# PE's matmuls in the attention loop: the scheduler's order or the source's

## The chip, the cores and the metric

The kernel runs on one core of a Trainium2 chip. The metric is the time of one execution on the device, in microseconds (us). Engines are named as in the profile: PE (matmul, with PEld for its weight loads), DVE (vector), ACT (scalar), POOL (GpSimd) and SP (DMA issue).

## The reference

Three stages follow one another: attention with pooled queries, a mixture of experts with top-1 routing and a skip rule, and a gated feed-forward layer.

```python
B, H, S, D = 4, 8, 1152, 64
q_pool = q.reshape(B, H, S // 2, 2, D).mean(axis=3)
scores = scale * q_pool @ k.transpose(0, 1, 3, 2)
attn = exp(scores - max(scores)); attn /= sum(attn) + 1e-9
x = (attn @ v), heads side by side            # 2304 x 512
x = x + gate * relu(x @ w1[e]) @ w2[e]        # rows with x @ w_skip > 0, e = argmax of x @ w_gate
out = (silu(x @ gate2) * (x @ val2)) @ out2   # d_ff 1536
```

All results are float32. To keep that precision on PE, operands of most products are split in a high and a low part (fp32r); the product with v and some small ones use plain fp32.

## The kernel before

Attention works on 16 pairs of heads, p = 0 to 15 (four pairs to a batch). For a pair, keys are cut in NC = 9 chunks of 128, queries (576 after pooling) in two halves n of 288, and a tile of scores is one (head, chunk, half).

The main loop, `for p in range(NP)` at line 786, is a software pipeline. It makes a list `main` of what pair p itself needs and a list `sides` of work for other pairs, and `spread` (line 24) emits both in one sequence: main pieces have whole positions, the pieces of a side are set evenly between two positions, and all are sorted.

Main pieces:

- `qk(p, h, c, n)`, lines 670 and 671: two fp32r matmuls (s) into a buffer of the PSUM pool ps_s (three buffers), then ACT's exp (line 674) into P[c], an SBUF tile with five buffers. In the source's order c runs from 0 to 8, and in a chunk (h, n) = (0,0), (0,1), then `values`, then (1,0), (1,1).
- `values`: for c = 2, 4, 6, 8 the products with v (`pv`, line 694, tile o) of chunks c-2 and c-1, eight fp32 matmuls; for c = 0 the four of the last chunk of the pair before. The matmul of head 0 writes partitions 0 to 63 and that of head 1 partitions 64 to 127, each a tile of 128x64 of PE, so the two can run side by side. At c = 4 the row sums of the pair before (`sums`, line 710, tile sm) come ahead of them.
- `evac(p - 1)`, line 702, on ACT after c = 0; `rowsum`, line 685, adds P to acc on POOL.

Side pieces:

- `m_pieces(p + 1)`: 27 score tiles of 128x384 for the row maxima (`m_tile`, mx, line 641), each reduced by DVE (line 643), and m_row, m_fin (mt, line 654, and line 655).
- `t_pieces(p + 2)`: transposes of k (tk, line 595, three at a time, copied out by ACT in lines 598 and 600) and of q (tq, line 608; lines 614 and 619 on ACT).
- `split_pieces(p + 3)`: the high and low parts of k and q (ACT and POOL), and its loads.
- In pairs from 4 on, Route: `rows(t)` (xr, lines 284 and 286; DVE lines 289 to 295; a store of the tile by SP, line 298; its SBUF tile xrs has one buffer), two tiles in pairs 4, 8, 12 and three in pairs 5, 9, 13; one-hot, softmax and rank in pairs 6, 10, 14 and near them, and scatters on POOL.
- In pairs 3 to 14, `Convert.decode` of weights stored as 64-bit floats (ACT lines 136 and 137, DVE lines 138 to 142), with a PSUM buffer; and in pair 15 the lists and loads for the experts, with the weight splits of lines 456 and 457.

mx, mt, tk, tq, sm, xr, and the PSUM tiles of decode and of the routing all take buffers of one pool, ps_m (three buffers); o has one tile of two banks of its own.

The instructions are emitted in this sequence, but Tile's scheduler sets the order on each engine: it plays the program through with its own cost model, and on each engine takes, of what it holds ready, the instruction emitted first. Where the next one in the source isn't ready by that model, a later one goes ahead. On the chip each engine then executes its list in order. Inside `tc.manual_schedule()` the order of emission is kept instead; the start of attention (`ramp`) and the experts (`moe`) are inside such regions, with all engines. The main loop isn't.

Of the kernel before, what the change touches and what calls it, by code (L numbers as in the profile page):

```python
# [20 lines left out]
ET = mybir.EngineType  # L21


def spread(main, sides):
    ev = []
    for i, f in enumerate(main):
        ev.append((i, 0, len(ev), f))
    for j, (pieces, a, b) in enumerate(sides):
        pieces = list(pieces)
        for i, f in enumerate(pieces):  # L30
            ev.append((a + (b - a) * (i + 0.5) / len(pieces), 1 + j, len(ev), f))
    for e in sorted(ev, key=lambda e: e[:3]):
        e[3]()
# [3 lines left out]
def body(ctx, tc, q, k, v, w_skip, w_gate, w1, w2, m2_gate, m2_val, m2_out, out):  # L37
# [433 lines left out]
    def attention(st):  # L471
# [186 lines left out]
        def m_pieces(p):  # L658
            r = [lambda i=i, j=j: m_tile(p, i // 5, i % 5, j) for i in range(9) for j in range(3)]
            r.insert(17, lambda: m_row(p, 0))  # L660
            r.insert(20, lambda: m_fin(p, 0))
            return r + [lambda: m_row(p, 1)]


        def qk(p, h, c, n):
            s = s_[p]
            cs = slice(c * 128, (c + 1) * 128)
            ns = slice(64 * h + n * 288, 64 * h + (n + 1) * 288)
            ps = ps_s.tile([128, 512], FP, tag="s", name="s")
            nc.tensor.matmul(ps[:, 0:288], s["ks"][:, h, cs], s["qsh"][:, h, ns], start=True, stop=False)  # L670
            nc.tensor.matmul(ps[:, 0:288], s["ks2"][0:69, h, cs], s["qsl"][0:69, h, ns], start=False, stop=True)  # L671
            if h == 0 and n == 0:
                s["P", c] = pp.tile([128, 2, 2, 288], FP, tag="P", name="P")
            i = nc.scalar.activation(s["P", c][:, h, n], ps[:, 0:288], AF.Exp, scale=0.5 / float(D) ** 0.5)  # L674
            if (h, c, n) == (0, 0, 0):
                mark[p] = i.ins.name

        def rowsum(p, c):
            s = s_[p]
            if c == 1:  # L680
                s["acc"] = accs[p % 2]
            if c:
                eng = nc.vector if p == last and c <= ACD else nc.gpsimd
                a = s["acc"][:].rearrange("p (h n c) -> p h n c", h=2, n=2)
                i = eng.tensor_tensor(a, s["P", 0][:] if c == 1 else a, s["P", c][:], op=ALU.add)  # L685
                if eng is nc.gpsimd:
                    mark["sum"] = i.ins.name

        def pv(p, c, n):
            s = s_[p]  # L690
            if c == 0 and n == 0:
                s["o"] = ps_o.tile([128, 2, 512], FP, tag="o", name="o")
            for h in range(2):
                nc.tensor.matmul(s["o"][h * 64:(h + 1) * 64, n, 0:288], s["vt"][:, h, c, :], s["P", c][:, h, n, :],  # L694
                                 start=c == 0, stop=c == NC - 1)
# [5 lines left out]
        def evac(p):  # L701
            nc.scalar.activation(xview(p), s_[p]["o"][:, :, 0:288], AF.Copy)

        def sum_up(p, src, first=True, last=True):
            if first:
                s_[p]["sm"] = ps_m.tile([128, 512], FP, tag="m", name="sm")
            for h in range(2):
                for n in range(2):
                    o = h * SQ + n * 288
                    nc.tensor.matmul(s_[p]["sm"][n * 64:(n + 1) * 64, 0:288], ones[:, 32 - 16 * h:96 - 16 * h], src[:, o:o + 288],  # L710
                                     start=first and not h, stop=last and h == 1)
# [7 lines left out]
        def sums(p):  # L719
            sum_up(p, s_[p]["acc"][:])  # L720
            sum_out(p)
            del s_[p]
# [58 lines left out]
        def sum_part(c):  # L781
            s = s_[last]
            src = s["acc"][:] if c == PEC - 1 else s["P", c][:].rearrange("p h n c -> p (h n c)")
            sum_up(last, src, c == PEC - 1, c == NC - 1)

        for p in range(NP):
            main = []
            for c in range(NC):
                pcs = [(p, c - 2), (p, c - 1)] if c and c % 2 == 0 else [] if c else [(p - 1, NC - 1)]
                for n in range(2):  # L790
                    if p or (c, n) not in early:
                        main.append(lambda c=c, n=n: qk(p, 0, c, n))

                def values(c=c, pcs=pcs):
                    if p and c == 4:
                        sums(p - 1)
                    for pc in pcs:
                        if pc[0] >= 0:
                            pv(*pc, 0)
                            pv(*pc, 1)  # L800
                main.append(values)
                main.append(lambda c=c: qk(p, 1, c, 0))
                if c == 0 and p:
                    main.append(lambda: evac(p - 1))

                def tail(c=c):
                    qk(p, 1, c, 1)
                    if p < last or c < PEC:
                        rowsum(p, c)
                main.append(tail)  # L810
            n = len(main)
            sides = []
            if not p:
                sides.append((split_pieces(2) + [lambda: load(3)], n * 0.6 / 9, n * 2 / 9))
            if p + 1 < NP:
                sides.append((m_pieces(p + 1), 0, n * 8.6 / 9))
            if p:
                sides.append(([lambda: m_fin(p, 1)], 1.5, 1.5))
            if p + 2 < NP:
                sides.append((t_pieces(p + 2, qs=False), n * 1.8 / 9, n * (5.2 if p else 6) / 9))  # L820
                sides.append((t_pieces(p + 2, ks=False), n * (5.2 if p else 6) / 9, n * (7 if p else 8) / 9))
            if p + 3 < NP:
                if p:
                    load(p + 3)
                sides.append((split_pieces(p + 3), n * (5.4 if p else 6.4) / 9, n * 8.6 / 9))
            if p + 1 < NP:
                load_v(p + 1)
            if p and p % HP == 0:
                routes.append(Route(p // HP - 1, routes[-1].scatters if routes else ()))
                bp = routes[-1].pieces()  # L830
            if p >= HP and p % HP < 2:
                rw = [lambda t=t, r=routes[-1]: r.rows(t) for t in range(G)]
                sides.append((rw[2:], 0, n * 4 / 9) if p % HP else (rw[:2], n * 5.2 / 9, n * 8.9 / 9))
            if p > HP and p % HP:
                cut = [0, *(CUT if p < last - 2 else CUL), len(bp)]
                sides.append((bp[cut[p % HP - 1]:cut[p % HP]], n * (4.5 if p == last - 2 else 1) / 9, n * (8.9 if p < last else 2.5) / 9))
            if 0 <= p - CP0 < 2 * len(first):
                if not (p - CP0) % 2:
                    cp = conv0.pieces(first[(p - CP0) // 2])
                    sides.append((cp[:1], n * 0.3 / 9, n * 0.3 / 9))  # L840
                    sides.append((cp[1:2], n * 6.5 / 9, n * 6.5 / 9))
                else:
                    sides.append((cp[2:], n * 3 / 9, n * 3 / 9))
            if p == last:
                sides.append(([list_a], n * 0.2 / 9, n * 0.2 / 9))
                sides.append(([lambda: load_w("A", 0, "r1", (), range(NFG - 1))], n * 1.5 / 9, n * 1.5 / 9))
                sides.append(([lambda: load_w("A", 0, "r1", (), range(NFG - 1, NFG))], n * 4.6 / 9, n * 4.6 / 9))
                sides.append(([lambda: load_ids("A", 0, routes[-1].scatters), lambda: gather("A", 0, 0)], n * 2.6 / 9, n * 3.5 / 9))
                pair = lambda i: psum[0]("xt")[:].rearrange("p (c n) -> p c n", c=2)
                sides.append(([lambda c2=c2: xt("A", 0, 0, c2, pair) for c2 in range(2)], n * XA / 9, n * 8.8 / 9))  # L850
                sides.append(([lambda g=g: split("r1", g, nc.gpsimd if g in AP1 else nc.vector) for g in range(3)], n * SA / 9, n * 8.8 / 9))
                sides.append(([lambda c=c: sum_part(c) for c in range(PEC - 1, NC - 1)], n * 8.3 / 9, n))
            spread(main, sides)
        sum_part(NC - 1)
        for n in range(2):
            pv(last, NC - 1, n)
# [331 lines left out]
    with ExitStack() as st:  # L1188
        routed = attention(st)
# [35 lines left out]
```

## Time and profile before

| what | us |
|---|---|
| median of 3 runs | 1247.16 (1246.89 to 1249.86) |
| the profiled execution, its own time | 1245.98 |
| its span, first to last instruction | 1244.4 |
| main loop, first to last evac | 70.6 to 592.4 |
| PE busy in the span | 1183.8 |

The span is 1.58 us shorter than that execution's own time, and the execution is 1.18 us under the median. Times in the rows are us from the start of the span. A matmul's end in the profile is modelled, since matmuls overlap; the distance from one start to the next is what it costs PE.

### The profile page before, as it was taken

The numbers are of one execution on the slowest core, as the hardware profiler recorded it, in microseconds if no ns is written. First come the engines' busy times: TensorE is split into PE (matmuls) and PEld (weight loads), VectorE is DVE, ScalarE is ACT, GpSimd is POOL, SyncE is SP. The second block draws the span as 40 slices with busy tenths as digits, with TensorE's granted clock in tenths as the row PEclk, the third lists the DMA queues.
The fourth block names the chain that finished last, engine by engine and source line by source line (L and its number), as shares of the span: only waits on it lengthen the run. The fifth ranks groups of instructions, "written<-read, shape, count | busy, mean of one in ns | idle before, by whom it ended". The sixth has DMA issues, their size and how long they took to land. (4 is left out here: it accounts for less than half of the span.)

```text
span 1244.4 us, 19070 instructions
## 1 busy us (share of the span) xinstructions
PE 1183.8 (95%) x6950; PEld 968.2 (78%) x6950; DVE 697.8 (56%) x1379; ACT 631.3 (51%) x1440; POOL 549.1 (44%) x328
## 2 busy tenths in 40 slices
PE   5999999999999999998789987999999999999998
PEld 3777776667776777675678876788898999989997
DVE  5555565655656565664756584927447374443333
ACT  5777775777757786654245375635223141221111
POOL 5878886779857997572332353202001020100000
PEclk9899999999999999998999998999999999999999
DMA  6311122111222111003486683522102020000012
GB/s 187 84 58 58 58 75 92 41 59 58 83 68 75 59 56 46 15 19 86 130 274 203 205 283 107 167 71 68 34 18 86 1 78 24 18 1 1 10 68 76
DMA packets 76618, 99.48 MB, mean 80 GB/s; under 512 B 6600, under 2 KB 50760, under 8 KB 76490
## 3 DMA queue, kind: packets, MB, share of 16 engines
q1 hardware_dynamic: 73290, 91.05, 22.9%
q0 software_dynamic: 3200, 6.86, 1.7%
q8 instruction: 64, 1.05, 0.3%
q14 instruction: 64, 0.52, 0.2%
HBM read 84.71 MB, written 12.53 MB: 78 GB/s over the span
## 5 line engine op out<-in xcount | busy, mean ns | idle before, releaser
L643 DVE TENSOR_REDUCE m<-mx 128x1 f32<-128x384 f32 x432 | 228.8, 555 | 178.2 <-PE mx L641 175.0
L685 POOL TENSOR_TENSOR acc<-acc,P 128x1152 f32<-128x1152 f32 x106 | 281.7, 2658 | 79.5 <-ACT P L674 43.0
L1115 PE MATMUL g<-xh,wc 128*128 128x384 f32 x1152 | 303.9, 337 | 2.0 <-ACT xh L1103 2.0
L674 ACT ACTIVATE P<-s 128x288 f32<-128x288 f32 x576 | 212.4, 411 | 107.4 <-PE s L671 101.1
L1115 PEld LDWEIGHTS g<-xh,wc 128*128 128x128 f32 x1152 | 208.3, 188 | 8.8 <-ACT xh L1103 7.5
L694 PE MATMUL o<-P,vt 128*64 128x288 f32 x1152 | 207.7, 424 | 2.3 <-ACT P L674 2.3
L1115 PE MATMUL g<-xl,wc 128*128 128x384 f32 x576 | 194.5, 338 | 0.0
L670 PE MATMUL s<-qsh,ks 128*128 128x288 f32 x576 | 180.9, 322 | 2.0 <-ACT P L674 1.3
L641 PE MATMUL mx<-ks,qsh 128*128 128x384 f32 x480 | 169.5, 382 | 4.6 <-DVE lp L295 3.4
L147 POOL TENSOR_TENSOR wc<-ct,wc 128x512 fp32r<-128x512 f32 x30 | 41.7, 1402 | 290.9 <-ACT wc L146 227.9
L671 PE MATMUL s<-qsl,ks 69*128 69x288 f32 x576 | 169.7, 302 | 0.0
L1142 PE MATMUL o<-wc,ah 128*128 128x512 f32 x432 | 137.4, 395 | 3.2 <-ACT ah L1129 3.2
L670 PEld LDWEIGHTS s<-qsh,ks 128*128 128x128 f32 x576 | 110.4, 192 | 33.9 <-issue 22.3
L694 PEld LDWEIGHTS o<-P,vt 128*64 128x64 f32 x1152 | 84.3, 137 | 61.7 <-issue 22.8
L1126 DVE TENSOR_TENSOR sg<-sg,g 128x384 f32<-128x384 f32 x72 | 39.8, 552 | 147.1 <-PE g L1115 133.4
L641 PEld LDWEIGHTS mx<-ks,qsh 128*128 128x128 f32 x480 | 87.6, 193 | 44.4 <-issue 17.4
L671 PEld LDWEIGHTS s<-qsl,ks 69*128 69x128 f32 x576 | 110.5, 192 | 0.0
L1115 PEld LDWEIGHTS g<-xl,wc 128*128 128x128 f32 x576 | 108.4, 188 | 2.1 <-DVE xl L1104 0.3
L1124 ACT ACTIVATE sg<-g 128x384 f32<-128x384 f32 x72 | 35.1, 488 | 143.9 <-PE g L1115 143.9
L1142 PEld LDWEIGHTS o<-wc,ah 128*128 128x128 f32 x432 | 79.6, 188 | 20.3 <-ACT ah L1129 6.6
L1129 ACT ACTIVATE ah<-sg 128x384 fp32r<-128x384 f32 x72 | 37.6, 522 | 107.9 <-DVE sg L1126 107.9
L1142 PE MATMUL o<-wc,al 128*128 128x512 f32 x216 | 85.5, 396 | 0.6 <-DVE al L1130 0.5
(277 smaller groups left out, 1676.6 us busy)
## 6 DMA issues: line engine op xcount, KB each, us to landing
r<-in_moe_w_dram SPq DMA_DIRECT2D x28, 512.0 KB
vt<-in_v_dram SPq DMA_DIRECT2D x16, 576.0 KB
kt<-in_k_dram SPq DMA_DIRECT2D x15, 576.0 KB
qraw<-in_q_dram SPq DMA_DIRECT2D x32, 256.0 KB
xT<-in_moe_w_dram SPq DMA_DIRECT2D x14, 512.0 KB
r<-in_moe_w_gate_dram SPq DMA_DIRECT2D x12, 512.0 KB
r<-in_moe_w_val_dram SPq DMA_DIRECT2D x12, 512.0 KB
r<-in_moe_w_out_dram SPq DMA_DIRECT2D x12, 512.0 KB
```

Source lines behind the costliest of these rows:

```text
L147: eng.tensor_tensor(w[:, 1], t[:], w[:, 0].bitcast(FP), op=ALU.subtract)
L641: nc.tensor.matmul(ps[:, 0:384], s["qsh"][:, g, c * 128:(c + 1) * 128], s["ks"][:, g, js], start=i == 0, stop=i == len(pr) - 1)
L643: nc.vector.tensor_reduce(s["m3"][:, 5 * h + t, j:j + 1], ps[:, 0:384], axis=AX, op=ALU.max)
L670: nc.tensor.matmul(ps[:, 0:288], s["ks"][:, h, cs], s["qsh"][:, h, ns], start=True, stop=False)
L671: nc.tensor.matmul(ps[:, 0:288], s["ks2"][0:69, h, cs], s["qsl"][0:69, h, ns], start=False, stop=True)
L674: i = nc.scalar.activation(s["P", c][:, h, n], ps[:, 0:288], AF.Exp, scale=0.5 / float(D) ** 0.5)
L685: i = eng.tensor_tensor(a, s["P", 0][:] if c == 1 else a, s["P", c][:], op=ALU.add)
L694: nc.tensor.matmul(s["o"][h * 64:(h + 1) * 64, n, 0:288], s["vt"][:, h, c, :], s["P", c][:, h, n, :], start=c == 0, stop=c == NC - 1)
L1115: nc.tensor.matmul(ps[:], w[:, a, fs], b[:], start=n == 0, stop=n == 3 * KD - 1)
L1126: nc.vector.tensor_tensor(sg[:], sg[:], vv[:], op=ALU.mult)
L1129: nc.scalar.activation(ah[:], sg[:], AF.Copy)
L1142: nc.tensor.matmul(ps[:], a[:, us], w[:, b, :], start=n == 0, stop=n == 3 * GF - 1)
```

## The change

PE's instructions in the main loop go out in the order of emission; DVE, ACT, POOL and SP stay with the scheduler. No instruction is added or taken away, and what follows the loop (the last `sum_part`, `pv`, `evac`) stays outside the region.

```diff
             src = s["acc"][:] if c == PEC - 1 else s["P", c][:].rearrange("p h n c -> p (h n c)")
             sum_up(last, src, c == PEC - 1, c == NC - 1)
 
+        steady = tc.manual_schedule(engines={ET.PE})
+        steady.__enter__()
         for p in range(NP):
             main = []
             for c in range(NC):
...
             spread(main, sides)
+        steady.__exit__(None, None, None)
         sum_part(NC - 1)
         for n in range(2):
             pv(last, NC - 1, n)
```

## Rows read from the trace of the kernel before

**Rows 1.** The page, busy time of the engines over the span.

```profile
PE 1183.8 (95%) x6950; PEld 968.2 (78%) x6950; DVE 697.8 (56%) x1379; ACT 631.3 (51%) x1440; POOL 549.1 (44%) x328
```

**Rows 2.** Source line 702 (evac): duration in ns, then first and last start.

```profile
L702 ACT ACTIVATE xT<-o x16: 652/652/653, 70.6 to 592.4; 128x576 f32<-128x576 f32 x16
```

**Rows 3.** Busy time by stretch, evac to evac: pairs 3, 4, 5, 6.

```profile
135.00:167.20 32.20, 32.20 (x213) 24.20 (x214) 19.00 (x38) 25.06 (x65) 26.81 (x13) 1.00 0.19 56
167.20:202.90 35.70, 35.70 (x233) 26.16 (x234) 21.62 (x50) 25.39 (x65) 28.69 (x14) 1.00 0.23 73
202.90:243.40 40.50, 38.30 (x243) 27.45 (x244) 22.77 (x56) 25.36 (x66) 25.30 (x12) 1.00 0.21 68
243.40:278.80 35.40, 35.40 (x219) 23.72 (x220) 22.16 (x55) 25.82 (x67) 27.34 (x13) 1.00 0.21 66
```

Columns: stretch, length, busy us (and instructions) of PE, PEld, DVE, ACT, POOL, the granted clock of PE as a share of 2.4 GHz, DMA share, GB/s.

**Rows 4.** Timeline of PE (start, length, instruction), pair 3 at c = 2.

```profile
138.87 2.16 PE L694 MATMUL o<-P,vt 128*64 128x288 f32 x16
140.96 0.45 PE L595 MATMUL tk<-idr,khl 128*128 128x128 f32 x3
```

**Rows 5.** Timeline of PE, pair 3, second half.

```profile
153.15 1.19 PE L694 MATMUL o<-P,vt 128*64 128x288 f32 x6
...
155.21 0.71 PE L694 MATMUL o<-P,vt 128*64 128x288 f32 x4
155.84 0.44 PE L641 MATMUL mx<-ks,qsh 128*128 128x384 f32 x1
156.22 1.19 PE L694 MATMUL o<-P,vt 128*64 128x288 f32 x6
157.33 0.40 PE L670 MATMUL s<-qsh,ks 128*128 128x288 f32 x1
...
158.50 0.70 PE L694 MATMUL o<-P,vt 128*64 128x288 f32 x2
159.13 0.28 PE L608 MATMUL tq<-idr,qhl 128*128 128x128 f32 x1
...
163.28 1.19 PE L694 MATMUL o<-P,vt 128*64 128x288 f32 x8
164.40 0.40 PE L670 MATMUL s<-qsh,ks 128*128 128x288 f32 x1
```

**Rows 6.** Timeline of ACT, the same stretch; in brackets idle before, and its end.

```profile
153.25 0.59 ACT L619 ACTIVATE qsl<-tq 64x512 fp32r<-64x512 f32 x1
153.87 0.41 ACT L674 ACTIVATE P<-s 128x288 f32<-128x288 f32 x1
...
158.79 0.41 ACT L674 ACTIVATE P<-s 128x288 f32<-128x288 f32 x1
159.45 0.55 ACT L614 ACTIVATE qsh<-tq 64x128 fp32r<-64x128 f32 x2 [0.25 <-PE tq L608]
...
160.31 1.01 ACT L674 ACTIVATE P<-s 128x288 f32<-128x288 f32 x3
```

**Rows 7.** Timeline of DVE in pair 4: a decode between reduces.

```profile
171.82 0.43 DVE L138 TENSOR_SCALAR cv<-r 128x256 int32<-128x256 int32 x1
...
175.09 0.56 DVE L643 TENSOR_REDUCE m<-mx 128x1 f32<-128x384 f32 x1 [0.25 <-PE mx L641]
...
177.18 0.42 DVE L142 SCALAR_TENSOR_TENSOR t<-cmk,cv 128x256 f32<-128x256 f32 x1
```

**Rows 8.** Timeline of PE in pair 5, after its second row tile.

```profile
211.23 1.19 PE L694 MATMUL o<-P,vt 128*64 128x288 f32 x8
213.37 0.59 PE L641 MATMUL mx<-ks,qsh 128*128 128x384 f32 x2 [0.95 <-DVE lp L295]
...
215.01 0.45 PE L595 MATMUL tk<-idr,khl 128*128 128x128 f32 x3
```

**Rows 9.** Timeline of all engines in pair 15, the longest wait of ACT.

```profile
568.51 1.06 ACT L456 ACTIVATE khl<-xT 128x1024 fp32r<-128x1024 f32 x1 [4.36 <-DMA xT<-in_moe_w_dram]
...
569.92 0.70 PE L694 MATMUL o<-P,vt 128*64 128x288 f32 x2 [2.00 <-ACT P L674]
```

## The prediction

> **What bounds the kernel now.** I read the page first, then the 16 pairs of the main loop one by one, then the timelines of PE, ACT and DVE inside three pairs.
>
> The page puts PE at 95% busy [rows 1]. That share does not say that PE runs without loss: ends of matmuls are modelled, so a PE that waits half a microsecond between two starts still counts as busy. What it loses is read from starts. The loop's milestones are the sixteen evac instructions [rows 2]: from 70.6 to 592.4 us, 15 intervals, 34.8 us each on average. Plain pairs (1, 2, 3, 7, 11) take 32.1 to 32.3 us, pairs 4, 8 and 12 (two token tiles of Route.rows) 35.7, pairs 5, 9 and 13 (three tiles) 38.2 to 40.5, pairs 6 and 10 (one-hot, softmax, rank) 35.3 to 35.4; one of each kind stands in [rows 3]. In a plain pair ACT is busy 25.06 of 32.2 us and POOL 26.81, so neither is a hard limit over a pair; each can be one over a stretch.
>
> The source order of PE follows from spread: main pieces at whole positions, side pieces at fractions. A values piece at even c emits its eight o matmuls without a break. Where the scheduler kept that, the run of eight (16 records, two per fp32 matmul) takes 2.09 us [rows 4]. In the second half of a plain pair it did not keep it: the runs of c=6 and c=8 stand in seven parts [rows 5], because mx, s and tq were judged not ready and o was at hand. Pairs 1 to 13 all have such a tail. Followed through all pairs, the source order has 98 runs of fp32 matmuls (o, sm, xr) in attention; the order on PE before has 191. So the change does move something: o stops filling waits.
>
> **What the change saves.** A run of 2 records (one matmul, half of a head pair) takes 0.63 us (158.50 to 159.13), and so does one of 4 records (155.21 to 155.84); 6 records take 1.11 us (156.22 to 157.33), and 8 take 1.12 (163.28 to 164.40) [rows 5]. A matmul split from its partner on the other 64 columns therefore costs as much as the two together, and each new run costs a fixed part. The seven runs take 1.11 + 0.63 + 1.11 + 0.63 + 0.64 + 0.62 + 1.12 = 5.86 us (the end of the first at 154.26, the fifth, 159.85 to 160.49, and the sixth, 162.19 to 162.81, are not shown); two runs of eight take 2 x 2.09 = 4.18 [rows 4]. That is 1.7 us less PE time per tail; going in and out of a run adds about 0.2 us at its neighbours, five times, another 1.0. Upper bound: 2.7 us for each of 13 tails, 35 us in all, if nothing PE then meets makes it wait.
>
> The Trainium skill (TensorEngine Tiling (Array Packing), Tiling Modes, Key Properties) says that changing the tiling mode drains TensorE. The trace agrees that a change from 128-column to 64-column tiles costs, and by that rule alone fewer runs must be faster; that is the first rival below.
>
> **What it costs: walking the tail in source order.** I keep the durations of [rows 5] and [rows 6] and let PE wait at each instruction. After mt, the next in source order is mx. All three ps_m buffers are held; the first comes free when ACT's qsl ends, 153.25 + 0.59 = 153.84 [rows 6]. PE, free at 153.1, stands until 153.9: in the trace those 0.8 us are o's. The next s needs the P that ends at 154.28; s, tq x4 and mx follow, and o's run of eight starts at 155.2 and ends with the next s at 157.3. In the trace that s is at 157.33 [rows 5]: no gain so far, since the saving went into waits. Then mx, tq and s go by 158.2; mx needs the reduce of the one buffer not held by tq (about 158.65, estimated from 157.65 for the last mx and the 1.05 us explained below); s needs P of 158.79, so 159.25; two mx until 160.2; the next s wait for the P's of 160.31 and after, at a pitch of 0.30 us [rows 6]; the last s ends at 161.87; o's run of eight lasts from 161.95 to 164.05. The trace has that next s at 164.40 [rows 5]. Gain 0.35 us, where the upper bound was 2.7. What hid the old waits was o, and without that cover they cost 2.3 us. Ten tails (pairs 1, 2, 3, 5, 6, 7, 9, 10, 11, 13): -3.5 us. Bounds: +0.5 (each wait slips by a little more) to -2.7 each.
>
> **The first halves.** In plain pairs the source order is kept already there: nothing. In pairs 4, 8 and 12 a decode holds one ps_m buffer from 171.82 to 177.60 [rows 7]. With two buffers left, an mx occupies one for about 1.05 us (an estimate: 0.56 for the reduce [rows 7] and some 0.5 for the matmul and the two handovers) and a tk for 1.4. Walked as above, PE stands before the second, third and fifth mx, for 0.3 to 0.5 us each time and again before the last ones, and ends the stretch 1.1 us later than the trace has it. Their tails, with a row tile inside, come out at -0.1. So +1.0, three times: +3.0. Bounds 0 to +2 each.
>
> In pairs 5, 9 and 13 a row tile holds two of the three ps_m buffers until DVE's lp is done (xrs has one buffer, so DVE also waits for the store of the tile before), and mx stands until 213.37; meanwhile PE runs eight records of o [rows 8]. In source order mx and two s stand ahead of the whole o run, so all eight matmuls come after 213.4: tk, at 215.01 in the trace [rows 8], comes at 215.7 to 216.4. The third tile costs some tenths more. I take +1.5, three times: +4.5; bounds 0 and +3 (twice the o time that covered a wait). What is queued behind the waiting mx is s, and so ACT's exp and POOL's sums; ACT is busy for 25.36 of the 40.5 us of pair 5 [rows 3], so it can take them late and the delay is PE's own.
>
> Pairs 6 and 10: four more runs than in a plain pair are saved, but one-hot and decode hold a buffer in turn; the walk ends 0.1 us earlier. -0.2 for both. Pairs 0, 14 and 15 lose two or three split runs each with few waits: -0.5 each, -1.5.
>
> DVE, ACT, POOL and SP keep their instructions; only when they are served changes. Nothing is added to a DMA queue.
>
> **Sum.** -3.5 + 3.0 + 4.5 - 0.2 - 1.5 = +2.3 us. The profiled execution took 1245.98 us, 1.2 below the median of the three runs, 1247.16. 1245.98 + 2.3 = 1248.3, and from the median 1249.5; I give 1249. About 0.3%, 3.7 us, is what a measurement of this kernel can tell from no change.
>
> **Rivals.**
> A. The saving wins. ACT's order adapts, P's and ps_m buffers come free earlier than in my walk, and half of the 2.7 us stays: 13 x 1.35 = 17.5 us, about 1230. For it: seven runs, where two would do, in every tail, and PE the engine that everything waits for. Against: the waits in the walk end on P and qsl, ACT work that does not move, and ACT idles only once, for 0.25 us, from 153.25 to the P's of 160.31 [rows 6]. It decides once the waits per tail fall below 1.3 us.
> B. The buffers decide: slower. Place: the first halves with a decode or a row tile. Price at twice my walk, as each mx that stands also delays the next reduce: 3 x 2 + 3 x 3 + 2 x 1.5 = 18 us, with tails at zero, about 1264. For it: the scheduler moved o just where DVE was late, and the trace says that it really was late. Against: in plain first halves the source order runs without a visible wait. It decides from about 1.5 us more per such pair.
> C. The last pair. PE waits there from o at about 567.5 to 569.92 because ACT stands for 4.36 us before a weight split whose DMA has not landed [rows 9]. If the scheduler, seeing other PE times, puts that split after the next exps, some 4 us go (1242); if it puts it earlier, as much is added (1253).
>
> **Chances and range.** Saving and waits cancel to within some 6 us: 0.40. A 0.25, B 0.25, C 0.10, half each way. Faster by over 0.3%: A, half of C, nothing else: 0.28, adjusting C down as 4 us barely passes. Slower by over 0.3%: B, half of C, and a quarter of the first case, 0.40. Same: 0.32. The range takes in half of A's spread and most of B's: 1234 to 1262. The forecast's own range is 1243 to 1255.
>
> **What would show it.** In the profile after, o stands in PE's timeline in runs of 16 records in every pair, with mx, s and tq right behind waits on DVE and ACT. Plain pairs take 31.5 to 32.3 us; pairs 4, 8, 12 about 36.5; pairs 5, 9, 13 one to two us more than now; 6 and 10 about 35. If plain pairs drop to 31 or less, A is right and my walk overstates waits. If pairs 4 to 6 grow by over 2 us each, B. If only the stretch after 556 moves, C. I would be wrong above all if ACT and DVE do their work in another order than before, since I kept theirs.

## The result: 1 per cent slower, most of it in four of the sixteen pairs

The changed kernel takes 1257.58 us (median of 7 runs, 1253.27 to 1265.47), the kernel before 1246.89 us beside it (7 runs, 1243.56 to 1249.86): a ratio of 1.0102, 95% interval 1.0068 to 1.0136. The forecast was 1249 with a range of 1234 to 1262; the sign of its sum held, and its size, +2.3 us, was too small. The median lies in that range, but outside the 1243 to 1255 that the forecast gave as its own.

The profiled execution of after took 1265.41 us, one of the two longest of the seven, with a span of 1263.8 us and a mean granted clock of 0.970. The quickest of the seven had 0.978. So what the profile shows is the change at its dearest; the median is some 8 us below it.

The page of after, PE's busy line, then the group of the evac instructions (duration in ns, first and last start):

```profile
PE 1167.7 (92%) x6950; PEld 973.3 (77%) x6950; DVE 700.2 (55%) x1379; ACT 631.1 (50%) x1440; POOL 551.8 (44%) x328
```

```profile
L702 ACT ACTIVATE xT<-o x16: 650/650/655, 73.2 to 611.4; 128x576 f32<-128x576 f32 x16
```

Against [rows 1] PE has the same 6950 instructions and is busy for 16.1 us less, in a span 19.4 us longer: it works less and waits more. Against [rows 2] the fifteen intervals of the loop grew from 521.8 to 538.2 us, 16.4 us of the 19.4. Another 2.6 us lie ahead of the first evac, where the clock was at half speed for 3.4 us longer than before; a later kernel whose pair 0 is left alone (e12) has 72.8 us there, against 73.2, and half speed for as long, so they are not put down to the change.

The lengths of the pairs in us, each worked out from two starts of evac (the last six columns are experiments, told below):

| pairs | before | after | e3 | e4 | e5 | e8 | e11 | e12 |
|---|---|---|---|---|---|---|---|---|
| 2 | 32.3 | 32.3 | 32.3 | 32.3 | 32.3 | 39.3 | 32.3 | 32.3 |
| 3, 7, 11 (decode) | 32.3 | 32.6 to 32.7 | 32.6 to 32.7 | 32.3 | 32.6 to 32.7 | 39.0 to 39.9 | 32.3 | 32.6 to 32.7 |
| 4, 8, 12 | 35.7 | 36.3 | 36.2 to 36.3 | 35.7 | 36.2 to 37.8 | 41.8 to 41.9 | 35.7 | 35.7 |
| 5 / 9 | 40.5 / 39.5 | 45.1 / 44.7 | 38.8 / 38.8 | 38.0 / 38.0 | 42.1 / 42.1 | 43.7 / 43.7 | 38.0 / 38.0 | 38.0 / 38.0 |
| 13 | 38.2 | 40.5 | 40.6 | 38.2 | 43.8 | 44.2 | 38.2 | 38.2 |
| 6 / 10 | 35.4 / 35.4 | 38.0 / 35.3 | 37.8 / 36.9 | 35.4 / 35.4 | 37.5 / 35.3 | 40.2 / 40.2 | 35.4 / 35.4 | 35.4 / 35.3 |
| 14 | 28.8 | 27.5 | 27.5 | 28.8 | 27.5 | 35.7 | 27.5 | 27.5 |

Pairs 5, 9, 13 and 6 carry +14.8 us of the 16.4; pair 14 gives 1.3 back.

**A plain tail.** After, stretches from evac to evac: pairs 3, 4, 5, 6 and 10 (columns as in [rows 3]).

```profile
137.80:170.44 32.64, 31.30 (x213) 23.57 (x214) 19.27 (x38) 24.80 (x66) 27.41 (x13) 1.00 0.19 55
170.44:206.69 36.25, 33.92 (x233) 26.20 (x234) 21.68 (x50) 25.50 (x65) 28.00 (x14) 1.00 0.24 71
206.69:251.83 45.14, 39.82 (x243) 29.92 (x244) 23.30 (x56) 25.41 (x65) 26.01 (x12) 0.89 0.19 61
251.83:289.79 37.96, 35.45 (x219) 25.54 (x220) 22.34 (x55) 25.77 (x67) 27.09 (x13) 0.91 0.20 62
403.36:438.64 35.28, 32.59 (x219) 24.10 (x220) 22.35 (x55) 25.65 (x66) 27.12 (x13) 1.00 0.22 66
```

Two things answer to [rows 3]. PE, busy for every microsecond of pair 3 before, is idle for 1.34 of 32.64. And in pairs 5 and 6 the granted clock, 1.00 in every pair of 1 to 14 before, is 0.89 and 0.91.

Timeline of PE in after, the second half of pair 3; subtract 2.8 us to lay it beside [rows 5]:

```profile
155.86 0.29 PE L671 MATMUL s<-qsl,ks 69*128 69x288 f32 x1
156.70 0.45 PE L641 MATMUL mx<-ks,qsh 128*128 128x384 f32 x1 [0.54 <-ACT qsl L619]
157.13 0.40 PE L670 MATMUL s<-qsh,ks 128*128 128x288 f32 x1
...
158.16 2.16 PE L694 MATMUL o<-P,vt 128*64 128x288 f32 x16
160.25 0.40 PE L670 MATMUL s<-qsh,ks 128*128 128x288 f32 x1
160.49 0.30 PE L671 MATMUL s<-qsl,ks 69*128 69x288 f32 x1
160.63 0.34 PE L641 MATMUL mx<-ks,qsh 128*128 128x384 f32 x1
161.61 0.28 PE L608 MATMUL tq<-idr,qhl 128*128 128x128 f32 x1 [0.65 <-ACT qsl L619]
...
165.51 2.16 PE L694 MATMUL o<-P,vt 128*64 128x288 f32 x16
167.60 0.40 PE L670 MATMUL s<-qsh,ks 128*128 128x288 f32 x1
```

The timeline of ACT in after, the same stretch, answers to [rows 6]:

```profile
156.05 0.59 ACT L619 ACTIVATE qsl<-tq 64x512 fp32r<-64x512 f32 x1
156.67 0.41 ACT L674 ACTIVATE P<-s 128x288 f32<-128x288 f32 x1
...
159.77 1.19 ACT L614 ACTIVATE qsh<-tq 64x512 fp32r<-64x512 f32 x2
160.96 0.59 ACT L619 ACTIVATE qsl<-tq 64x512 fp32r<-64x512 f32 x1
```

The seven runs of o are two of sixteen records, as forecast. Where o stood between, PE waits twice for a ps_m buffer that ACT's qsl gives back: mx 0.84 us after the matmul ahead of it (155.86 to 156.70; such a pair of starts is 0.13 to 0.14 us apart elsewhere), tq 0.98 us after mx (160.63 to 161.61; elsewhere 0.18). Less the usual distances, that is 1.5 us of waiting, and the tail of pair 3 ends 0.4 us later than before; so the five runs saved were worth about 1.1 us. Pair 2, which has no decode, has the first of these waits too, but its tq follows mx after 0.18 us (128.31 to 128.49); only a later mx stands, for 0.4 us, and the pair takes 32.3 us as before.

**Pair 5.** Timeline of PE in after; it answers to [rows 8].

```profile
209.71 0.29 PE L671 MATMUL s<-qsl,ks 69*128 69x288 f32 x1
211.75 0.41 PE L641 MATMUL mx<-ks,qsh 128*128 128x384 f32 x1 [1.74 <-DVE lp L295]
...
215.24 0.72 PE L595 MATMUL tk<-idr,khl 128*128 128x128 f32 x3
217.29 0.66 PE L641 MATMUL mx<-ks,qsh 128*128 128x384 f32 x1 [1.33 <-DVE lp L295]
...
219.16 4.11 PE L694 MATMUL o<-P,vt 128*64 128x288 f32 x16
223.20 0.54 PE L595 MATMUL tk<-idr,khl 128*128 128x128 f32 x3
```

What lp waits for stands in DVE's timeline of the same stretch:

```profile
210.92 0.56 DVE L292 TENSOR_TENSOR xr<-xr,rs 128x384 f32<-128x384 f32 x1 [1.67 <-DMA xd<-xr]
...
216.47 0.56 DVE L292 TENSOR_TENSOR xr<-xr,rs 128x384 f32<-128x384 f32 x1 [0.88 <-DMA xd<-xr]
```

There is one xrs, so the next row tile is written only when the store of the last one has landed; DVE stands 1.67 us, and mx behind it stands 2.03 us from start to start (1.55 before, and there too no o ran in it: o covered the second wait alone). The sixteen o records that come after the second wait take 4.04 us (219.16 to 223.20), where a run of sixteen took 2.09 in [rows 4]. The reason is in the clock. Busy time by stretch in after, two short stretches inside pairs 5 and 6, the granted clock third from the end:

```profile
213.30:223.50 10.20, 8.87 (x39) 6.03 (x37) 2.89 (x9) 2.10 (x6) 2.69 (x1) 0.50 0.21 75
274.70:281.50 6.80, 6.65 (x26) 3.73 (x27) 1.62 (x8) 3.55 (x10) 5.24 (x3) 0.50 0.28 87
```

0.50 is the lower of the two levels, 1.2 of 2.4 GHz. Pair 9 has such a stretch of 10.2 us as well, pair 13 one of 3.4, each behind waits of PE; before, there is none from pair 1 to pair 14.

**Pair 6.** Timeline of PE in after, ahead of the second of those stretches:

```profile
271.89 0.33 PE L654 MATMUL mt<-idr,m 128*128 128x128 f32 x1
273.08 0.18 PE L324 MATMUL rk<-ohb,tri 128*128 128x40 bf16 x1 [0.86 <-ACT qsl L619]
...
274.68 0.75 PE L608 MATMUL tq<-idr,qhl 128*128 128x128 f32 x4 [0.49 <-DVE m L643]
```

Pair 10 has the same first wait (1.19 us from start to start in both), a second of 0.68 us where pair 6 has 0.79, and no drop of the clock: 35.3 us where pair 6 took 38.0.

**The last pair.** ACT's longest wait, the one that answers to [rows 9], in ACT's timeline of after:

```profile
587.89 1.06 ACT L456 ACTIVATE khl<-xT 128x1024 fp32r<-128x1024 f32 x1 [3.97 <-DMA xT<-in_moe_w_dram]
```

It is as it was (4.36 us before), and pair 15 takes 35.8 us instead of 36.0.

### The profile page after: what moved, and what is told of

The parts are those of the page before. It is cut to its first block, busy times and chain, and to the rows that moved or that the text cites. A ratio compares the mean times of both kernels' runs of the same rounds, so it can differ in the third digit from the quotient of the medians.

```text
span 1263.8 us, 19086 instructions
## 1 busy us (share of the span) xinstructions
PE 1167.7 (92%) x6950; PEld 973.3 (77%) x6950; DVE 700.2 (55%) x1379; ACT 631.1 (50%) x1440; POOL 551.8 (44%) x328
## 5 line engine op out<-in xcount | busy, mean ns | idle before, releaser
L674 ACT ACTIVATE P<-s 128x288 f32<-128x288 f32 x576 | 215.9, 412 | 136.0 <-PE s L671 128.7
L641 PE MATMUL mx<-ks,qsh 128*128 128x384 f32 x480 | 174.4, 387 | 22.0 <-ACT qsl L619 8.6
L670 PE MATMUL s<-qsh,ks 128*128 128x288 f32 x576 | 183.8, 326 | 8.8 <-ACT P L674 6.3
L147 POOL TENSOR_TENSOR wc<-ct,wc 128x512 fp32r<-128x512 f32 x30 | 41.9, 1410 | 290.9 <-ACT wc L146 227.8
L694 PE MATMUL o<-P,vt 128*64 128x288 f32 x1152 | 165.6, 429 | 0.0
L670 PEld LDWEIGHTS s<-qsh,ks 128*128 128x128 f32 x576 | 112.0, 194 | 41.8 <-issue 22.3
L641 PEld LDWEIGHTS mx<-ks,qsh 128*128 128x128 f32 x480 | 90.3, 196 | 46.2 <-ACT qsl L619 14.1
```

The costliest lines, as they stand in the source:

```text
L147: eng.tensor_tensor(w[:, 1], t[:], w[:, 0].bitcast(FP), op=ALU.subtract)
L641: nc.tensor.matmul(ps[:, 0:384], s["qsh"][:, g, c * 128:(c + 1) * 128], s["ks"][:, g, js], start=i == 0, stop=i == len(pr) - 1)
```

## The experiments

Theory 1: the loss sits in the pairs with router work, where o no longer covers PE's wait for the router rows, and where the clock falls behind that wait. Theory 2: the order costs a little in every pair. Ratios are to the kernel before, run beside each.

**e1 and e2: the order in part of the loop.** Both open and close the held order pair by pair:

```diff
-            spread(main, sides)
+            with tc.manual_schedule(engines={ET.PE}) if p not in (5, 9, 13) else ExitStack():   # e2: p in (5, 9, 13)
+                spread(main, sides)
```

> PE keeps the order of the source in all pairs but 5, 9 and 13, which go back to the scheduler's order. Theory 1: most of the loss sits in these three pairs, where PE in order stands behind the tiles of Route.rows. In the two profiles they grew by 4.6, 5.2 and 2.3 us of the 19 us that the loop grew by. Then this kernel is 2 to 6 us slower than before (ratio 1.001 to 1.005). Theory 2: order costs a little everywhere (decode buffers, tails, routing pairs), so leaving out three pairs of sixteen gives back a fifth: ratio 1.008.

> PE keeps the order of the source in pairs 5, 9 and 13 alone. Theory 1: 6 to 12 us slower than before (ratio 1.005 to 1.010), with PE's granted clock at half for some 10 us after the waits in these pairs, as in the profile after. Theory 2: about 2 us slower (1.002).

e1: 1258.19 us, 1.0063 (1.0045 to 1.0082). e2: 1256.36 us, 1.0055 (1.0040 to 1.0069). The three pairs alone carry half of the whole. The two ratios add up to about that of after; by the profiles the loops grew by 10.0 and 11.7 us, more together than the 16.4 of after, since pair 9 is long in both. In e2 pairs 5, 9 and 13 take 44.7, 42.9 and 41.8 us with 10.2, 6.8 and 6.8 us at half clock, where after has 45.1, 44.7 and 40.5 us with 10.2, 10.2 and 3.4: pair by pair, the time goes with the clock. e1, between its two expectations, is a partial miss for theory 1: pair 13 is back at 38.2 us, but pair 9, left to the scheduler, still takes 44.5 us, since mx there stands 2.01 us for lp (1.49 before) and 10.2 us at half clock follow. The store of xr ahead of it is issued 1.10 us into the pair, where before it was 0.73. So the pairs ahead of it move where the store meets it; the order inside pair 9 is not all.

**e3 and e4: without the wait for the store.** Two row tiles in turn, the second one a tile of t0 that is idle until pair 13; e3 is after with this line, e4 is before with it.

```diff
-            xr = xrs if xr is None else xr
+            xr = (xrs, t0[first[-1]])[t % 2] if xr is None else xr
```

> The changed kernel, and the row tile xr gets a second buffer (a weight tile that is not yet in use), so that DVE need not wait for the store of the tile before. Theory 1: the waits of 1.7 and 0.9 us of DVE for the store go, mx stands shorter, PE's clock stays high in pairs 5, 9, 13, which fall to about 40 us or less; 1247 to 1251. Theory 2: pairs 5, 9, 13 gain under 1 us each, 1255 or more. If the clock stays high although PE still waits over 1 us, the length of the wait decides.

> The kernel before with the second buffer for the row tile. In its trace DVE waits four times for the store, 4.4 us, and PE stands 1.3 us behind it in pairs 5 and 9 twice. Theory 1: 2 to 6 us faster than before (1241 to 1245), less than the same edit gives the changed kernel, since the scheduler covers part of the wait with o. Theory 2: the edit gives both kernels the same.

e3: 1253.32 us, 1.0032 (1.0017 to 1.0046), between its two expectations. e4: 1243.25 us, 0.9946 (0.9931 to 0.9961), as expected. Pairs 5 and 9 of e3, busy time by stretch, and PE's wait for lp in the first of them (total, times, longest):

```profile
207.55:246.38 38.83, 35.73 (x243) 27.32 (x244) 23.18 (x56) 25.31 (x65) 25.99 (x12) 1.00 0.23 70
353.08:391.92 38.84, 35.75 (x243) 27.33 (x244) 23.19 (x56) 25.32 (x66) 25.96 (x12) 1.00 0.23 70
```

```profile
PE mx L641 <- DVE lp L295: 0.9, 1, 0.9
```

With the store out of the way the clock stays at 1.00, and source order costs 0.9 us a pair there (38.84 against 37.98 in e4). The wait for the store was in the kernel before as well: taken away there (e4), the same two pairs give back 40.5 + 39.5 - 2 x 38.0 = 4.0 us. Pair 13 does not move (40.6), so its loss has another source.

**e5: the wait kept, PE kept at work in it.** Twenty matmuls of the identity by itself, read by nobody, ahead of the two waiting mx of pairs 5, 9 and 13:

```diff
+            if p in (5, 9, 13):
+                def busy():
+                    ps = ps_s.tile([128, 512], FP, tag="s", name="busy")
+                    for i in range(20):
+                        nc.tensor.matmul(ps[:, 0:128], idr[:], idr[:], start=True, stop=True)
+                sides += [([busy], x, x) for x in (6.3, 10.8)]
             spread(main, sides)
```

> The kernel after, with 20 extra matmuls of the identity by itself (into a score buffer, read by nobody) put on PE ahead of the two matmuls of pairs 5, 9 and 13 that wait over 1.3 us for the router rows in pair 5 (1.74 and 1.33 us idle). The wait itself is left as it is: VectorE's work and the store of xr are the same. Theory 1 (the waits cost little by themselves, the granted clock that falls to half behind them costs the rest: 10.2 us at half clock in pairs 5 and 9, 3.4 in 13): PE has no idle stretch of over 1 us there, the clock stays at full speed in pairs 5, 9 and 13, and they take 41 to 42.5 us instead of 45.1, 44.7 and 40.5; the kernel is 4 to 8 us faster than after. Theory 2 (the order itself, with its waits, costs the time, and the lower clock is only seen beside it): pairs 5 and 9 stay within 0.7 us of 45 whatever the clock does, and the kernel is as slow as after or slower by the 120 extra matmuls.

Pairs 5 and 9 of e5, by stretch, and PE's timeline at the two places in pair 5:

```profile
207.75:249.89 42.14, 39.89 (x283) 31.80 (x284) 23.28 (x56) 25.30 (x66) 26.03 (x12) 1.00 0.21 65
357.81:399.88 42.07, 39.83 (x283) 31.73 (x284) 23.39 (x56) 25.30 (x65) 26.01 (x12) 1.00 0.21 65
```

```profile
210.78 0.30 PE L671 MATMUL s<-qsl,ks 69*128 69x288 f32 x1
210.91 2.35 PE L859 MATMUL busy<-idr 128*128 128x128 f32 x20
213.10 0.39 PE L641 MATMUL mx<-ks,qsh 128*128 128x384 f32 x1
...
215.90 2.42 PE L859 MATMUL busy<-idr 128*128 128x128 f32 x20
218.20 0.41 PE L641 MATMUL mx<-ks,qsh 128*128 128x384 f32 x1
219.25 2.16 PE L694 MATMUL o<-P,vt 128*64 128x288 f32 x16
221.34 0.46 PE L595 MATMUL tk<-idr,khl 128*128 128x128 f32 x3
```

mx comes no sooner (2.32 us after the matmul ahead, 2.03 in after), the clock stays at 1.00, o's run is back at 2.09 us (219.25 to the next start at 221.34), and pairs 5 and 9 take 42.1 us instead of 45.1 and 44.7. DVE's waits for the store are no shorter in sum (3.2 us against 2.6 in pair 5, 2.8 against 2.0 in pair 9). So at least 3.0 and 2.6 us of the loss there are the clock's, and at most 1.6 and 2.6 us remain for the waits (against 40.5 and 39.5). As a whole e5 is a miss: 1266.34 us, 1.0136 (1.0100 to 1.0173), not 4 to 8 us quicker. In pair 13, where mx waits for lp only once and for 0.86 us, most of the extra matmuls are plain work: 43.8 us instead of 40.5. And stretches at half clock came up in pair 8 and behind the loop that after's profile does not have.

**e6 and e7: without the decode's ps_m buffer.** e6 is after, e7 is before with the two row tiles and with source order in pair 14; both with

```diff
-                r.append(lambda i=i: self.decode(self.raw[a], t0[a], i, psum[0]("cv")))
+                r.append(lambda i=i: self.decode(self.raw[a], t0[a], i))
```

> The kernel after, with the decode's two intermediates in SBUF instead of a buffer of the three that the maxima (mx, mt) also use. Theory A (the buffers that the decode holds are what makes mx wait in the pairs with a decode): pairs 4, 8 and 12 fall from 36.3 to 35.4 or less, pairs 3, 7 and 11 from 32.6 to about 32.3, pair 6 loses its two waits of 1.19 and 0.79 us; in all 2 to 4 us faster than after. Theory B (mx waits because ACT, which makes qsh and qsl of the transposed halves, is behind): these pairs stay within 0.3 us of after, pair 6 at 37 to 38.

> The kernel before with two row tiles taken in turn for xr, the decode's intermediates in SBUF, and PE held to the order of the source in pair 14 alone (27.5 us in after, 28.8 before). If what the runs so far show adds up: the two row tiles give 6 us as alone, pair 14 another 1.0 to 1.3, the decode 0 to 3: a ratio to before of 0.990 to 0.994. If the gain of pair 14 came from its neighbours being in source order as well, or the decode in SBUF loads VectorE more than it frees, no better than the two row tiles alone (0.9946).

e6: 1275.44 us, 1.0231 (1.0195 to 1.0266). e7: 1263.39 us, 1.0130 (1.0103 to 1.0157). Both did more than was meant: with no buffer to bind it, the scheduler moved nearly all of the decode into the start-up and pairs 0 and 1; the stretch to the first evac and pair 1 grew from 70.6 + 32.1 to 85.3 + 39.9 us in e6 and to 86.6 + 39.6 in e7. As kernels they are no use, but their later pairs show the loop without a decode in it. Pairs 8 and 12 take 34.69 us in source order (e6) and 34.75 in the scheduler's (e7); pairs 3, 7 and 11 take 32.3 in both. (Pair 4 of e6 takes 36.2 us, but has 3.4 us at half clock.) So the 0.6 us that source order costs in pairs 4, 8 and 12, and the 0.4 us in 3, 7 and 11, are there only while a decode is. Whether it is the buffer it holds or its time on DVE, these two runs don't tell apart.

**e8: more splits instead of fewer.** e4's kernel with the o matmuls raised in the scheduler's priority, which scatters them:

```diff
-            for h in range(2):
+            with tc.high_priority(offset=60):
+              for h in range(2):
                 nc.tensor.matmul(s["o"][h * 64:(h + 1) * 64, n, 0:288], ...
```

> The kernel before with two row tiles in turn for xr and the o matmuls raised in the scheduler's priority, so that they are scattered through the loop in 297 runs instead of 188, 234 of them of an odd length instead of 100. Theory 1 (one more change between the 128-column and the 64-column matmuls costs PE about 0.34 us, a split head pair 0.3 us on top, by the rows of before): a hundred more runs cost 35 to 70 us of PE time, the kernel is 1.02 to 1.05 of before. Theory 2 (the changes are nearly free, since PE's weight loads and waits hide them, which would explain why 108 runs fewer in the order of the source saved nothing): within 1 per cent of the two row tiles alone (0.995 to 1.005 of before).

e8: 1337.74 us, 1.0722 (1.0687 to 1.0757), beyond both expectations. Pair 2, busy time by stretch, in the kernel before, and then in e8:

```profile
102.68:134.98 32.30, 32.30 (x213) 24.36 (x214) 17.23 (x33) 24.24 (x64) 26.94 (x13) 1.00 0.18 56
```

```profile
116.42:155.70 39.28, 38.89 (x213) 23.73 (x213) 17.34 (x33) 25.27 (x63) 26.87 (x13) 1.00 0.16 46
```

The same 213 matmul records, PE idle for at most 0.4 us, 7.0 us more. Counted in the two timelines, the runs of 64-column matmuls in this pair went from 10 to 21, those that split a pair of heads from 4 to 14: 0.6 us for each added run, more than the 0.54 of the forecast's upper bound (2.7 us for five). The tail of after gives back less: about 1.1 us for the five runs saved, 0.2 each. So theory 2 falls: the changes are not free.

**e9 and e10: ACT's qsl earlier.** The second copy of tq into qsh goes from ACT to VectorE, in e3's kernel (e9) and in e4's (e10):

```diff
-                if ts is None or i ^ sw == 0:
+                if (ts is None and not (p > 2 and i)) or (ts is not None and i ^ sw == 0):
```

> PE held to the order of the source, two row tiles in turn for xr, and the second of the two copies of tq into qsh moved from ACT to VectorE (from p 3 on), so that ACT reaches qsl about 0.6 us earlier in each tail. Theory 1 (the order saves PE 1.5 us of changes in each tail, and the wait for ACT's qsl, 0.83 and 0.99 us from start to start in pair 2, eats it): the plain pairs 1, 2, 3, 7, 10 and 11 come down by 0.7 to 1.5 us each, the kernel is 8 to 16 us faster than the same without this edit (1.0032 of before, 1253.3 us against 1249.3), so at 0.990 to 0.998 of before. Theory 2 (fewer changes save PE nothing; the waits are only where PE's spare time shows): the plain pairs stay at 32.2 to 32.7 and the kernel at 1.000 to 1.005 of before.

> The control: the kernel before with two row tiles and the same copy of qsh on VectorE, PE left to the scheduler. PE has no wait for qsl in the plain pairs of before (0.00 us idle in pair 2), so both theories expect no gain from it there: 0.993 to 0.997 of before, as the two row tiles alone (0.9946), or up to 0.5 per cent slower than that if VectorE comes late in pairs 5, 9 and 13.

e9: 1258.25 us, 1.0092 (1.0075 to 1.0108), 0.6 per cent behind e3 where a gain was expected. e10: 1251.80 us, 1.0036 (1.0022 to 1.0050), 0.9 per cent behind e4, more than the half per cent that was allowed for. Pairs 2 and 3 of e9 by stretch, then pair 3 of e10:

```profile
106.28:138.13 31.85, 30.78 (x213) 23.60 (x214) 19.00 (x37) 22.59 (x60) 27.05 (x13) 1.00 0.19 58
138.13:170.39 32.26, 30.86 (x213) 23.57 (x214) 20.92 (x42) 23.10 (x62) 27.43 (x13) 1.00 0.20 61
```

```profile
136.17:169.41 33.24, 33.24 (x213) 24.42 (x214) 21.02 (x42) 23.10 (x62) 28.34 (x14) 1.00 0.12 36
```

Against e3, with the clock at 1.00 in both, pairs 2, 3, 7 and 9 came down by 0.4 to 0.5 us, and pairs 4 and 8 went up by 0.1 to 0.2. Pair 2 has PE busy for 30.78 us, the least of any kernel here, with 1.07 us idle. The first wait is no longer for ACT: mx stands 1.09 us for DVE's qsl rows. As a whole e9 loses because 3.4 us at half clock stand in each of pairs 1, 5, 6, 10, 11, 12 and 13, where e3 has half clock in 6, 10 and 13 alone. In e10 the scheduler's order changed with the edit: pairs 3, 7 and 11 take 33.2 us with PE never idle, with eleven runs of 64-column matmuls, six of which split a pair of heads, instead of ten and four; pair 14 takes 31.9 with twelve runs instead of seven. So in pairs 3 and 7 the source order (32.3 us in e9) is here 1.0 us quicker than the scheduler's. Theory 1 is borne out in those pairs, at 0.4 to 0.5 us instead of 0.7 to 1.5; mostly the wait moves rather than goes.

**e11 and e12: the order where it does no harm.** e4's kernel, PE held to the source in pair 14 (e11), and in 1, 2, 3, 7, 11 and 14 (e12), by the `with` of e1.

> The kernel before with two row tiles, and PE held to the order of the source in pair 14 alone. If the 1.3 us of pair 14 (28.8 to 27.5) belong to that pair's order alone: 0.9936 of before, 1 us under the two row tiles; if its neighbours must be in that order as well, 0.9946, as without it. Neither result bears on the cause in pairs 5, 9 and 13, where this kernel's loop should be that of the two row tiles (38.0, 38.0 and 38.2 us).

> The kernel before with two row tiles, and PE held to the order of the source in the pairs without row tiles and one-hot alone: 1, 2, 3, 7, 11 and 14. Theory 1 (a tail in source order gives PE 1.5 us of changes back and waits as long for ACT's qsl, so it is neutral; the loss of after sits in the pairs with router work and in the clock behind their waits): pairs 1, 2, 3, 7 and 11 at 32.1 to 32.7, 14 at 27.5, no stretch at half clock in the loop, and the kernel within 2 us of the one with the order in pair 14 alone, 0.994 to 0.998 of before. Theory 2 (the order costs something in every pair, and waits of 0.8 to 1 us are enough for the clock to fall): a clock below full speed in some of these pairs, and 1.000 of before or more.

e11: 1242.43 us, 0.9960 (0.9943 to 0.9976); pair 14 takes 27.5 us, all other pairs are e4's. e12: 1244.68 us, 0.9963 (0.9946 to 0.9980); pairs 1 and 2 at 32.3, 3, 7 and 11 at 32.6 to 32.7, clock 1.00 from pair 1 to 14. Theory 1 holds: in plain pairs the order is neutral or costs 0.2 to 0.4 us, and without the router pairs nothing drops the clock in the loop. e11 settles that the gain of pair 14 is its own order's; as a whole the kernel shows none beyond e4. e4, e11 and e12 all beat both kernels; between e4 and e11 these runs can't tell.

## Why the prediction was right in sign and short in size

**Tails, -0.35 us each: too hopeful by about 0.6.** Pairs 1, 2, 3, 7 and 11 changed by +0.2, 0.0, +0.4, +0.4 and +0.4 us. The walk met the trace up to the first run of o: PE stands until 153.9 and the next s is at 157.3, it said; after's 156.70 and 160.25 are 153.90 and 157.45 on before's scale. The step that failed is the next one, "mx, tq and s go by 158.2": tq finds all three ps_m buffers held, one of them by a decode, and waits until ACT's qsl of the second big tq is done. The walk had charged neither; in pair 2, without a decode, that tq does not wait. The s behind the second run of o comes at 164.80 on that scale, not at 164.05. The saving itself is real, but smaller than its upper bound of 2.7: about 1.1 us in pair 3, where PE's busy time fell from 32.20 to 31.30 us. Rival A needed that saving to last, and PE spends it waiting for qsl. The Trainium skill (TensorEngine Tiling (Array Packing), Tiling Modes, Key Properties) says that changing the tiling mode drains TensorE. The trace of e8 agrees that the changes cost (7.0 us for 11 more runs); the conclusion that fewer of them must be faster did not hold here.

**Pairs 4, 8, 12, +1.0 each:** +0.6 measured, in the bounds. That it hangs on the decode is shown by pairs 8 and 12 of e6 and e7.

**Pairs 5, 9, 13, +1.5 each: the term that was mis-sized.** Measured +4.6, +5.2 and +2.3, above its bound of +3 in the first two. The mechanism was the one named: mx and what stands behind it wait for lp with no o to cover them. e5 puts the waits at 1.6 and 2.6 us at most, inside the bounds of 0 and +3, and without the store the order costs 0.9 (e3 against e4). What the walk left out is that the clock would fall behind the wait, at least another 3.0 and 2.6 us. It took all durations from a trace in which the clock never fell in these pairs. In pair 13 nothing waits for the store (e3 changes nothing there): mx waits once for lp, 0.86 us, where o ran before; the tail has waits of 1.19 and 1.10 us for ACT's qsl, then 3.4 us at half clock. How much each costs there was not measured by itself.

**Pairs 6 and 10, -0.1 each:** pair 10 came out at -0.1, pair 6 at +2.6, by the same order and the same first wait. The difference goes with the half clock, 6.8 us in pair 6 and none in pair 10; that it is the clock's was not tested there by itself.

**Pairs 0, 14, 15, -0.5 each:** 14 gave 1.3 (e11 shows that this is the order's), 15 0.2; pair 0 is not told apart from the clock's drops ahead of the loop.

**Sum.** By the profile the loop lost 16.4 us where +2.3 was forecast; the clock's share by e5 and by pairs 6 and 10 is 3.0 + 2.6 + 2.7, or 8.3 us, half of it. Rival B, buffers at twice the walk, is not what happened: pairs 4, 8 and 12 cost less than the walk, not more, and that its price of 18 us is near the 16.4 of the loop is chance. So it is in part luck that the median lies in the range: it fell in the part above 1255, which had been added for B. Rival C neither: [rows 9] stayed. (Its 1242 is worked out from 1245.98 and its 1253 from 1249; from 1249 both ways it is 1245 and 1253.) **Left open** is what decides whether a wait of PE is followed by half clock: pairs 6 and 10 differ with no difference in their instructions, and the runs of after spread by 12 us. Only the profiled execution shows which pairs had it, so how much of the median's 10.7 us is the clock's stays open too.

## What to carry to other kernels

An instruction order that removes mode changes or splits from PE pays only if what follows is ready: before counting the saving, read at each place what the filler covered, and give it the wait in full. A walk that lets PE stand for one to two microseconds at a time must also price the clock, at both levels, because the stretch behind the wait may run at half speed. And where a filler covers a wait, look first at the wait itself: the second row tile, one line, gained half a per cent, more than any order tried here.

## What the runs showed of the hardware

- Splitting the 64-column matmuls of o among 128-column ones cost 0.6 us of PE time per added run in e8: pair 2 went from 32.30 to 39.28 us with 11 more runs, ten of them splits of a pair of heads, and the same records.
- PE's granted clock fell to half for 3.4 to 10.2 us behind waits in which PE stood for 1.2 to 2.4 us with work on either side, and not behind like waits elsewhere (1.19 us in pair 10, 1.55 us in pair 5 of before). With twenty matmuls put into each of these waits, which did not end the first one in pair 5 sooner (2.32 us against 2.03), it stayed at 1.00 in pairs 5 and 9.
- One kernel's executions differ with the clock: of the seven of after, the two longest, 1265.41 and 1265.47 us, have the two lowest means, 0.970 and 0.971; the quickest, 1253.27 us, has 0.978.
